# Delta-rule attention and feed-forward on one core: the first two chunks rebuilt

## The chip, the cores and the metric

The kernel runs on one core of a Trainium2 chip. The metric is the device time of one execution in microseconds; lower is better. The engines named below are TensorE (PE, with its weight loads as PEld), VectorE (DVE), ScalarE (ACT), GpSimd (POOL) and SyncE (SP). SP does no arithmetic here: it issues DMAs, in order, and a DMA that has to wait holds up those behind it. ACT and POOL issue some DMAs as well.

## What is computed

Two blocks follow each other. The first is a delta rule: for each of 4 batches and 8 heads a 48 x 48 state is carried over 768 tokens. The second is a feed-forward network on the 3072 tokens with all heads side by side (384 columns).

```python
k_n = k / (np.linalg.norm(k, axis=-1, keepdims=True) + 1e-06)
for t in range(S):
    y[:, :, t] = np.einsum('bhd,bhde->bhe', q[:, :, t], state)
    v_old = np.einsum('bhde,bhd->bhe', state, kt)
    state = state + bt[:, :, :, None] * np.einsum('bhd,bhe->bhde', kt, vt - v_old)
...
h = x @ w_in                                # 384 -> 2048
g = h * (1.0 / (1.0 + np.exp(-1.702 * h)))
return (g @ w_out).astype(np.float32)       # 2048 -> 384
```

The inputs q, k, v and beta are float32. The two weight matrices are float64 in DRAM, and the kernel turns them into float32 itself.

## The kernel before

**Tiling.** The 768 tokens are cut into 6 chunks of 128. A *unit* is one chunk of one batch with its 8 heads; there are 24, and unit n is chunk n // 4 of batch n % 4. Two neighbouring units (n even and n + 1) are a *pair*: they share one xT tile of 256 tokens, on which the feed-forward works.

**A unit's work.** `normalize` divides k by its norm (in the loop: squares, the power and the product on POOL, the rest on DVE). `prepare` transposes k on PE (psT, copied to kT), forms the products of all keys with all keys (psG, copied to G) and sends all of G, 512 KB, to DRAM (Nd). From there SP reads back the 32 x 32 blocks of the diagonal (NT), so that each (batch, head, block) lies on a lane of its own. `invert` turns these blocks into the inverses of unit lower triangular matrices by substitution on DVE: a multiplication with beta, 15 steps of a product and a reduction, then two groups of four larger products and reductions. The result goes to DRAM and back once more (Yd, XB). Chunk 0 is inverted for four units at once (128 lanes), the later ones a pair at a time (64 lanes). `scores` transposes q (psT, QS), multiplies it and the state with the keys (psQ), subtracts the state's part from V and masks the scores M on POOL.

**The chain.** The 128 tokens of a unit are four blocks of 32. `together` does one hop: `solve` multiplies the inverse of a block with V (psU, copied by ACT to US), and `below` subtracts a solved block from the blocks under it (psR, subtracted from V on DVE by `rest`). A hop handles a solve of one unit and a below of another, so two or three units are under way at once. `queries`, `outputs` and `state` make the output (psY) and the new state (ST). ACT copies the output to xT and `last`, and six SP DMAs move `last` into xT.

**Feed-forward.** `hidden` is x @ w_in with the activation (ph, gT), 16 pieces of three products a pair; `written` is g @ w_out (po, o, and a DMA to the output), 8 pieces of two products a unit. Both are generators; finished pairs are put into `queue`, and pieces are drawn from it between the steps of the attention. A piece has a cost of 1.3, and the share of a unit is 15.6 to 20.8.

**Weights.** The two words of a double are fetched into w_out's own space (or a spare tile) and made into a float by DVE and ACT (`from_double`), in parts of 512 columns for w_in and 384 for w_out. In the first units POOL issues most of these loads, as places become free.

**Order.** For units -1 to 5 `slot` runs six groups of steps (for units 2 to 5 with a scheduler's freedom on DVE, ACT and PE); from unit 6 on `woven` runs with the program's order held. `warm` issues products of a constant, whose results are not used. The names that the later text uses stand in these lines:

```python
for n in range(-1, len(units) + 1):
    in_order[0], now[0] = n < HB or n >= W, n
    step = slot if n < W else woven
    step(n, 15.6 if n <= B else 18.8 if n <= B + HB else 20.8)
run(take(1e9))
```

Of the kernel before, what the change touches and what calls it, by code (L numbers as in the profile page):

```python
# [18 lines left out]
def kernel(  # L19
# [33 lines left out]
    GR = 6  # L53
    NTH = HB * C
    FQ = 4
    GB = 4

    W0, W1, WB = 3, 1, (1, 3, 5, 7, 8)
    NA = W0

    NW, NA0, NY, NB0 = 80, 3, 48, 6
    XR = DP - D
    W = 6
    NS = C * C + C
    assert S % C == 0 and H == 8 and D <= DP and DM == H * D == KC * 128
    assert B == 4 and B * H * NB == 128 and FC == 4 * FQ
# [40 lines left out]
    in_order, now = [False], [0]  # L107

    class Engine:
# [5 lines left out]
        def __getattr__(self, name):  # L115
            op = getattr(self.engine, name)
            return pinned(op) if in_order[0] else op

    vec, act, pe = Engine(nc.vector), Engine(nc.scalar), Engine(nc.tensor)

    for i in range(B):
        nc.vector.memset(KN[i][:, :, D:DP], 0.0)
        load(i, ((KN, k),))

    bI = cpool.tile([128, NC, BS], F32, name="bI")
    betas = beta.rearrange("b h (c k j) -> (b h) c k j", k=NB, j=BS)
    for blk in range(NB):
        nc.scalar.dma_start(out=bI[blk::NB], in_=betas[:, :, blk, :])


    ident = cpool.tile([128, 128], F32, name="ident")
    make_identity(nc, ident)
    half = cpool.tile([128, H], F32, name="half")
    nc.gpsimd.memset(half, 0.5)

    nc.gpsimd.memset(YB, 0.0)
    nc.gpsimd.affine_select(
        out=YB, in_=YB, compare_op=ALU.not_equal, fill=1.0, base=0,
        pattern=[[1, BS], [-1, BS]], channel_multiplier=0,
    )  # L140


# [5 lines left out]
    def warm(n, after=None):  # L148

        ps = ps_moe.tile([128, 256], F32, tag="moe", name="ps_warm")  # L150
        if after is not None:
            after(ps[:, 0:1], 0.0)
        for _ in range(n):
            pe.matmul(ps, lhsT=ones[:, 0:128], rhs=ones, start=True, stop=True)  # L154

    warm(NW)
    table = cpool.tile([128, 1], F32, name="table")
    nc.scalar.activation(table, ident[:, 0:1], ACT.Copy)

    w_in = cpool.tile([128, KC, DFF], F32, name="w_in")  # L160
# [3 lines left out]
    nc.gpsimd.memset(low, -896.0 * (1 << 23))  # L164

    def from_double(dst, raw, n, alone):

        lo, hi = raw[:, :, 0], raw[:, :, 1]
        ts, stt = vec.tensor_scalar, vec.scalar_tensor_tensor
        if alone:
            ts, stt = pinned(ts), pinned(stt)
        AND, OR = ALU.bitwise_and, ALU.bitwise_or
        E1 = 1 << 20
        p = dst.bitcast(I32)  # L180

        ts(p, hi, 0x7FF * E1, None, op0=AND)
        if alone:
            ts(p, p, -896.0 * E1, 0.0, op0=ALU.add, op1=ALU.max)
            ts(p, p, 255.0 * E1, 8.0, op0=ALU.min, op1=ALU.mult)
        else:
            act.activation(p, p, ACT.Relu, scale=8.0, bias=low)
        yield
        t = wk.tile([128, n], I32, tag="P", name="tmp")
        f = t.bitcast(F32)  # L190
        ts(t, hi, E1 - 1, E1, op0=AND, op1=OR)
        stt(out=f, in0=lo.bitcast(U32), scalar=2.0**-32, in1=t, op0=ALU.mult, op1=ALU.add)
        stt(out=p, in0=hi, scalar=-(1 << 31), in1=p, op0=AND, op1=OR)
        stt(out=dst, in0=f, scalar=2.0**-20, in1=dst, op0=ALU.mult, op1=ALU.mult)
        yield

    N_IN = 512
    parts_in = KC * DFF // N_IN
    n_parts = parts_in + FC

    x_rows = [
        (ct * DP + o, (ct * NP + i) * D, m, step)
        for ct in range(2)
        for o, i, m, step in ((0, 0, D, D), (D, KC, XR, XR))
    ]

    stages, taken, made, begun = {}, {}, [], {}  # L210

    def stage(part):

        if part < parts_in:
            at = part % (2 * KC) * 2 * N_IN
            return at, at + 2 * N_IN
        f = part - parts_in
        if f >= FC - 2:
            return None
        depth = 2 if f < 2 or f >= 8 else 4  # L220
        if f >= 12:
            depth = 1
        at = FC * DM // (2 if f < 2 else 1) - (f % depth + 1) * 2 * DM
        return at, at + 2 * DM

    def together_with(part):

        return list(range(part, part + (KC if part < 3 * KC else 1)))

    def free(part):  # L230
        places = [s for p in together_with(part) if (s := stage(p)) is not None]
        return all(s[1] <= a or b <= s[0] for s in places for a, b in taken.values())

    def fetch(part, dma):

        if part < parts_in:
            j, f0 = part % KC, part // KC * N_IN
            parts = together_with(part)
            shape, src = (len(parts), N_IN), moe_w_in[:, f0 : f0 + N_IN]
            dst = w_in[:, j : j + len(parts), f0 : f0 + N_IN]  # L240
        else:
            parts = [part]
            shape, src = (1, DM), moe_w_out
            dst = target(part)
        if src.dtype != F32:
            if (s := stage(part)) is None:
                raw = wk.tile([128, *shape, 2], I32, tag="xT", name="raw", bufs=3)
            else:
                words = slice(s[0], stage(parts[-1])[1])
                raw = w_out.rearrange("p f d -> p (f d)")[:, words].bitcast(I32)  # L250
                raw = raw.rearrange("p (j n o) -> p j n o", j=shape[0], o=2)
            for i, p in enumerate(parts):
                stages[p] = raw[:, i]
                if s is not None:
                    taken[p] = stage(p)
            dst = raw.bitcast(src.dtype).rearrange("p j n o -> p j (n o)")
        if part < parts_in:
            for i in range(len(parts)):
                for p, r, m, step in x_rows:
                    dma(out=dst[p : p + m, i], in_=src[r + (j + i) * step : r + (j + i) * step + m])  # L260
        else:
            r = (part - parts_in) * 128
            dma(out=dst if src.dtype == F32 else dst[:, 0], in_=src[r : r + 128, :])
        return parts

    def target(part):
        if part < parts_in:
            j, f0 = part % KC, part // KC * N_IN
            return w_in[:, j, f0 : f0 + N_IN]
        return w_out[:, part - parts_in, :]  # L270

    def begin(part):

        if part not in begun:
            if part >= parts_in:
                a, b = (part - parts_in) * DM, (part - parts_in + 1) * DM
                if any(taken[p][0] < b and a < taken[p][1] for p in stages if p in taken):
                    return
            dst = target(part)
            begun[part] = from_double(dst, stages[part], dst.shape[-1], part < NA)  # L280
            next(begun[part])

    def convert(part):
        if part in stages:
            begin(part)
            if staged:
                begin(min(staged))
            stages.pop(part)
            next(begun.pop(part))

            made.append(part)
            while made and (len(made) > 1 or part < NA or part >= n_parts - 8):
                taken.pop(made.pop(0), None)

# [20 lines left out]
    def normalize_first(b0, nb=HB):  # L315

        tt, ts = pinned(vec.tensor_tensor), pinned(vec.tensor_scalar)
        red, recip = pinned(vec.tensor_reduce), pinned(vec.reciprocal)
        stt = pinned(vec.scalar_tensor_tensor)
        mult, add = ALU.mult, ALU.add  # L320
        z = wk.tile([128, 4, nb, H], F32, tag="ksq", name="z", bufs=1)
        x, y, t, s = (z[:, i] for i in range(4))
        for b in range(nb):
            K = KN[(b0 + b) % len(KN)][:, :, 0:D]
            sq = wk.tile([128, H, D], F32, tag="G", name="sq", bufs=6)
            tt(sq, K, K, op=mult)
            red(s[:, b], sq, axis=AX.X, op=add)
# [8 lines left out]
        recip(s, s)  # L336
        for b in range(nb):
            K = KN[(b0 + b) % len(KN)][:, :, 0:D]
            tt(K, K, s[:, b].broadcast_to([128, H, D]), op=mult)

    def transposed(src, dst, early=False):

        pool_, tag = (ps_seq, "seq") if early else (ps_big, "big")
        psT = pool_.tile([128, NP, 128], F32, tag=tag, name="psT")
# [5 lines left out]
    def prepare(n):  # L350

        c, b = units[n]
        kn = KN[n % len(KN)]
        kT = wk.tile([128, NP, 128], F32, tag="kT", name="kT", bufs=6)
        transposed(kn, kT, c == 0)
        yield 0.6
        G = wk.tile([128, H, 128], F32, tag="G", name="G", bufs=6)
        pool_, tag = (ps_moe, "moe") if c == 0 and b % 2 else (ps_big, "big")
# [10 lines left out]
        else:  # L369
            vec.tensor_copy(G[:, 1::2], ps[1])  # L370

        Nd = dram.tile([H * NS], F32, tag="Nd", name="Nd", bufs=4)
# [16 lines left out]
    def invert(c, b0=0, nb=B):  # L389
# [6 lines left out]
        if c == 0:  # L396
            tt, red = pinned(tt), pinned(red)
# [535 lines left out]
```

## Time and profile before

| what | value |
|---|---|
| median of 3 runs | 825.57 us (823.43 to 826.2) |
| the profiled execution | 821.86 us |
| its span, first to last instruction | 819.8 us |
| mean granted TensorE clock | 0.952 |
| DMA | 55.96 MB in 147698 packets |
| xT DMAs of unit 0 / of unit 1 issued on SP from | 94.09 us / 118.27 us |
| dummy products on PE (`ps_warm`) | 152 + 108 |
| po, 128 x 384 | 704 + 64 records, two for each product |

How to read it: the busy share of an engine is a mean over the whole span, and stages with different limits are mixed in it. A matmul's record has its latency in it, so the price of one is better taken from a long row of them. An idle engine costs nothing unless others wait for it. The line number of a group is often that of a helper (L105 holds the program's order), so groups are told apart by their tiles.

### The profile page before, as it was taken

To read this page: it belongs to the slowest core of one execution; us is meant where nothing else is said; L and a number is where in the kernel's file an instruction comes from. 1 tells how busy PE (TensorE), PEld (TensorE's weight loads), DVE (VectorE), ACT (ScalarE), POOL (GpSimd) and SP (SyncE) were. 2 spreads that over 40 slices of the span, in tenths; PEclk is the share of its full clock that TensorE was granted. 3 is DMA by queue.
4 is the path that set the end of the run, shared out by engine and by line. 5 is a ranking of instruction groups with operands and counts; after the bars stand their busy time and mean duration, and the time that the engine had idled before them with its cause. 6 is when DMAs were issued, how large, how long until landed. Compare 5 with 4: busy or idle time off the path is not lost.

```text
span 819.8 us, 18780 instructions
## 1 busy us (share of the span) xinstructions
PE 768.8 (94%) x8100; PEld 577.4 (70%) x8100; DVE 483.0 (59%) x1037; ACT 230.7 (28%) x499; POOL 131.7 (16%) x138
## 2 busy tenths in 40 slices
PE   8429799889799999999999999999999999999998
PEld 7327688557676876867867867867768768677684
DVE  7797989787965675666667667666656730100000
ACT  2212543242232332322422322322322223212120
POOL 2013120322021222122123122212201000000000
PEclk9659889978979999999999999999999999999999
DMA  7986732721315123214204213213222020000000
GB/s 146 199 183 122 201 87 82 178 68 48 68 30 125 34 49 96 60 23 100 62 21 102 53 32 90 54 43 80 53 59 45 12 51 1 11 16 1 24 1 19
DMA packets 147698, 55.96 MB, mean 68 GB/s; under 512 B 114720, under 2 KB 143616, under 8 KB 147616
## 3 DMA queue, kind: packets, MB, share of 16 engines
q1 hardware_dynamic: 139872, 41.96, 24.0%
q0 software_dynamic: 2752, 10.62, 4.7%
q10 hardware_dynamic: 4992, 2.20, 1.0%
q8 instruction: 63, 1.03, 0.6%
q14 instruction: 19, 0.16, 0.1%
HBM read 33.13 MB, written 20.45 MB: 65 GB/s over the span
## 4 chain that ended last, share of the span: by engine, by line
PE 79%; DVE 6%; issue 6%; DMA 4%; SPq 2%; POOL 1%; ACT 1%; DVEq 0%; POOLq 0%; ACTq 0%
PE po L105 28%; PE ph L105 25%; PE psY L105 5%; PE psU L105 4%; PE psQ L105 3%; PE ps_warm L154 3%; PE ph L633 2%; PE psG L105 2%; PE psR L105 2%; DMA w_out<-in_moe_w_out_dram 2%; PE psT L105 1%; SPq L105 1%; DMA w_out<-in_moe_w_in_dram 1%; DVE tmp L105 1%; PE psG L362 1%
## 5 line engine op out<-in xcount | busy, mean ns | idle before, releaser
L105 PE MATMUL po<-w_out,gT 128*128 128x384 f32 x704 | 239.3, 490 | 0.0
L105 PE MATMUL ph<-xT,w_in 128*128 128x256 f32 x966 | 222.0, 384 | 0.3
L105 PEld LDWEIGHTS ph<-xT,w_in 128*128 128x128 f32 x966 | 180.3, 191 | 30.9 <-issue 2.3
L105 PEld LDWEIGHTS po<-w_out,gT 128*128 128x128 f32 x704 | 130.1, 190 | 82.6 <-issue 1.9
L105 DVE TENSOR_TENSOR V<-V,psR 64x384 f32<-64x384 f32 (+1 forms) x80 | 44.4, 556 | 194.8 <-PE psR L105 194.0
L105 DVE TENSOR_TENSOR P<-NT,YB 64x18 f32<-64x18 f32 (+25 forms) x171 | 82.3, 481 | 4.5
L105 ACT ACTIVATE gT<-ph 128x512 f32<-128x512 f32 x81 | 48.2, 595 | 115.9 <-PE ph L105 115.8
L105 DVE TENSOR_REDUCE YB<-P 64x6 f32<-64x18 f32 (+25 forms) x171 | 72.7, 425 | 5.5
L105 ACT COPY US<-psU 32x384 f32<-32x384 f32 x80 | 37.6, 470 | 131.9 <-PE psR L105 118.4
L528 POOL TENSOR_SCALAR_AFFINE_SELECT M<-M 128x1024 f32<-128x1024 f32 x24 | 29.8, 1240 | 226.6 <-DVE M L105 159.8
L105 PEld LDWEIGHTS psU<-V,XB 32*32 32x32 f32 x1280 | 45.9, 105 | 27.9 <-issue 20.5
L105 PE MATMUL psU<-V,XB 32*32 32x48 f32 x1280 | 54.3, 203 | 2.1 <-DVE V L105 2.1
L105 PE MATMUL psR<-US,G 32*32 32x48 f32 x1920 | 52.8, 203 | 0.0
L633 PE MATMUL ph<-xT,w_in 128*128 128x128 f32 (+1 forms) x282 | 47.0, 321 | 1.6 <-DMA xT<-last 1.6
L105 PEld LDWEIGHTS psR<-US,G 32*32 32x32 f32 x1920 | 44.6, 105 | 0.5 <-issue 0.5
L633 PEld LDWEIGHTS ph<-xT,w_in 128*128 128x128 f32 x282 | 40.3, 198 | 5.7 <-issue 2.4
L154 PE MATMUL ps_warm<-ident 128*128 128x256 bf16 x152 | 22.8, 318 | 16.7 <-DVE ps_warm L105 14.4
L90 POOL DMA_DIRECT2D KN<-in_k_dram x14 | 13.4, 955 | 153.1 <-PE psY L105 102.0
L308 POOL TENSOR_TENSOR rn<-ssq,half 128x8 f32<-128x8 f32 x17 | 36.9, 2169 | 2.9 <-DVE ssq L306 2.9
L105 ACT COPY o<-po 128x384 f32<-128x384 f32 x22 | 10.5, 479 | 77.7 <-PE po L105 55.8
L154 PEld LDWEIGHTS <-ident 128*128 128x128 bf16 x152 | 17.1, 114 | 21.0 <-issue 14.6
L105 DVE TENSOR_TENSOR P<-NT 64x256 f32<-64x256 f32 (+7 forms) x36 | 30.3, 841 | 0.3
(144 smaller groups left out, 871.0 us busy)
## 6 DMA issues: line engine op xcount, KB each, us to landing
Nd<-G SPq DMA_DIRECT2D x20, 512.0 KB, 3.5
w_out<-in_moe_w_out_dram POOLq DMA_DIRECT2D x14, 384.0 KB, 3.7
QP<-in_q_dram SPq DMA_DIRECT2D x24, 192.0 KB, 3.9
V<-in_v_dram SPq DMA_DIRECT2D x24, 192.0 KB, 3.0
out_dram<-o SPq DMA_DIRECT2D x24, 192.0 KB, 1.9
w_out<-in_moe_w_in_dram SPq DMA_DIRECT2D x18, 192.0 KB, 5.2
NT<-Nd SPq DMA_DIRECT2D x24, 128.0 KB, 2.6
Yd<-YS SPq DMA_DIRECT2D x24, 128.0 KB, 2.5
```

The lines of the kernel that those rows point to most:

```text
L90: dma(out=dst[n % len(dst)][:, :, 0:D], in_=src[b, :, c * C : (c + 1) * C, :].rearrange("h p d -> p h d"),)
L105: return lambda *a, **kw: tc.keep_in_program_order(op(*a, **kw))
L154: pe.matmul(ps, lhsT=ones[:, 0:128], rhs=ones, start=True, stop=True)
L308: nc.gpsimd.tensor_tensor(rn, ssq, half, op=ALU.pow)
L362: pe.matmul(ps[h % 2][:, h // 2], lhsT=kT[r, h // 2, :], rhs=kT[r, h // 2, :], start=True, stop=True,)
L528: nc.gpsimd.affine_select(out=self.M, in_=self.M, compare_op=ALU.is_gt, fill=0.0, base=0, pattern=[[0, H], [1, 128]], channel_multiplier=-1,)
L633: pe.matmul(ph[:, u], lhsT=w_in[:, j, f * 128 : (f + 1) * 128], rhs=xT[:, j, t], start=(j == 0), stop=(j == KC - 1),)
```

## The change

The steps up to unit 8 are written out by hand, and the program's order is held for them on PE, DVE, ACT, POOL and SP. From unit 7 on `woven` runs as before. In detail:

- The keys of all four units of chunk 0 are normalized in one go. Their squares are made by ACT.
- For chunk 0 only the diagonal blocks of the key products are formed first (psD, 32 x 32, in `diagonal`) and sent through DRAM, a quarter of the bytes; G is formed afterwards and stays on the chip.
- Chunk 1 is inverted for its four units at once, on 128 lanes, as chunk 0 is.
- Units 0 and 1, then 2 and 3, 4 and 5, 6 and 7 run as pairs of chains (`hops`): eight hops, in which one unit's solve stands beside the other's below. Between the hops stand pieces of feed-forward (`feed`) and of conversion (`fill`).
- The conversion works on pieces of 768 columns (256 of w_in for all three parts, or two parts of w_out), then of 384. Loads are issued by SP (in part by POOL for the first two quarters of w_in) when a named piece is done.
- x @ w_in of units 0 to 3 comes first; g @ w_out begins when all weights are converted.
- `spend` keeps no debt while the queue of feed-forward is empty. ACT makes the copies for which it shared the work with DVE.
- gT has eight buffers where it had four; spare ones hold some of the tiles of the first units.

```diff
+    def diagonal(b, D_):
+        kT = kTs[b]
+        ps = [ps_seq.tile([128, NP, BS], F32, tag="seq", name="psD") for _ in range(2)]
+        for h in range(H):
+            r = slice(h % 2 * 64, h % 2 * 64 + D)
+            for blk in range(NB):
+                u = slice(blk * BS, (blk + 1) * BS)
+                pe.matmul(
+                    ps[h % 2][u, h // 2, :], lhsT=kT[r, h // 2, u], rhs=kT[r, h // 2, u],
+                    start=True, stop=True,
+                )
+        for e in range(2):
+            act.activation(D_[:, e::2, :], ps[e], ACT.Copy)
...
+    fetches = {
+        ("in", 1): lambda: fetch_in(2),
+        ("in", 3): lambda: fetch_in(3),
+        ("in", 5): lambda: (fetch_out(0), fetch_out(1)),
+        ("in", 7): lambda: (fetch_out(2), fetch_out(3), fetch_out(4), fetch_out(5)),
+        ("out", 3): lambda: (fetch_out(6), fetch_out(7), fetch_out(9), fetch_out(12)),
+        ("out", 5): lambda: fetch_out(8),
+        ("out", 7): lambda: (fetch_out(10), fetch_out(11), fetch_out(13)),
+        ("out", 9): lambda: fetch_out(14),
+        ("out", 12): lambda: fetch_out(15),
+    }
...
     def spend(cost):
-        debt[0] += cost
+        debt[0] = debt[0] + cost if queue else 0.0
...
+    for b in range(B):
+        sync(
+            out=NT[b * NB * H : (b + 1) * NB * H].rearrange("d i k -> d (i k)"),
+            in_=Nds[b].rearrange("(d r) -> d r", r=BS * BS),
+        )
...
+    fill(8)
+    for b in range(B):
+        gram(b)
+        warm(NA)
+    pair = [new_step(n) for n in range(B)]
+    inverting = invert(0)
...
+    run(inverting)
+    fill(5)
+    def hops(a, b):
+        yield [(a, 0)], []
+        for blk in range(NB - 1):
+            yield [(b, blk)], [(a, blk)]
+            yield [(a, blk + 1)], [(b, blk)]
+        yield [(b, NB - 1)], []
...
+    path = hops(*pair[:2])
+    for i in range(2 * NB):
+        together(*next(path))
+        fill(1)
+    for s in pair[:2]:
+        put_out(s)
+        fill(2)
...
+    ffn.append(hidden(xTs[0], gTs[0], slice(0, NTH), 1.3))
+    path = hops(*pair[2:])
+    for i in range(2 * NB):
+        together(*next(path))
+        feed()
+        fill(2)
+    for s in pair[2:]:
+        put_out(s)
+        feed()
+        fill(2)
...
+    for n in range(B, 2 * B):
+        for _ in keys(n):
+            feed()
+            fill(3)
+    requests(3)
+    while len(ffn) > 2:
+        feed()
+        fill(3)
+    run(converting)
+    inverting = invert(1)
+    pair = [new_step(n) for n in (B, B + 1)]
+    for i in range(20):
+        ahead_of(inverting, 1 + i % 4 // 3)
+        feed()
...
+    run(inverting)
+    for n in (8, 9):
+        for _ in keys(n):
+            feed(1 if n == 8 else 0)
...
+    chain(*pair, lambda i: feed())
+    enqueue(2)
...
+    def more(i):
+        ahead_of(inverting, 1)
+        feed(2)
+    chain(*pair, more)
+    enqueue(3)
...
+    queue.extend(ffn)
+    for n in range(7, len(units) + 1):
+        woven(n, 20.8)
     run(take(1e9))
```

## The prediction

> **What bounds the kernel now.** I read the page's busy times and slices first, then a table of stages, then the chain of waits, and the order of instructions of both programs last.
>
> ```profile
> span 819.8 us, 18780 instructions
> PE 768.8 (94%) x8100; PEld 577.4 (70%) x8100; DVE 483.0 (59%) x1037; ACT 230.7 (28%) x499; POOL 131.7 (16%) x138
> PE   8429799889799999999999999999999999999998
> DVE  7797989787965675666667667666656730100000
> PEclk9659889978979999999999999999999999999999
> ```
>
> TensorE is full from about 230 us on. Before that VectorE is the fuller engine and TensorE is partly kept warm by dummy products. The table by stage (columns: PE, PEld, DVE, ACT, POOL busy, clock, DMA share, GB/s):
>
> ```profile
> 0.00:67.00 67.00, 38.04 (x295) 30.74 (x296) 56.93 (x138) 15.67 (x32) 12.70 (x31) 0.72 0.96 177
> 67.00:112.00 45.00, 39.03 (x679) 32.84 (x677) 36.93 (x83) 21.70 (x43) 11.30 (x17) 0.89 0.63 154
> 112.00:176.00 64.00, 57.00 (x690) 42.18 (x689) 57.00 (x123) 22.83 (x54) 13.93 (x18) 0.97 0.40 101
> 176.00:230.00 54.00, 48.57 (x456) 36.98 (x457) 43.41 (x100) 15.93 (x33) 6.52 (x6) 0.82 0.28 63
> 289.00:347.00 58.00, 57.89 (x655) 43.44 (x654) 35.96 (x77) 17.11 (x39) 11.41 (x10) 1.00 0.26 62
> ```
>
> In the last row two units take 58 us and VectorE has 36 us of work in them (40 in the 59 us before). That number decides below. The chain of waits fixes the rest of the run, and the price of feed-forward work:
>
> ```profile
> 398.55 2.07 PE psY L105 x48
> ...
> 775.08 20.72 PE ph L105 x96
> 795.80 20.66 PE po L105 x64
> ```
>
> 398.55 is unit 10's output; 421.25 us follow, all TensorE-bound. 20.72/96 and 20.66/64 make a piece of feed-forward work (three products of ph, or two of po) 1.29 us, and a pair's feed-forward 41.4 us. The start, from the timeline, SP's queue and the DMA table:
>
> ```profile
> 31.00 1.22 DVE L105 TENSOR_TENSOR NT<-NT,bI 128x1024 f32<-128x1024 f32 x1 [3.11 <-DMA NT<-Nd]
> 57.97 7.58 PE L154 MATMUL ps_warm<-ident 128*128 128x256 bf16 x48 [14.36 <-DVE ps_warm L105]
> 67.44 0.86 PE L105 MATMUL psU<-V,XB 32*32 32x48 f32 x16
> 69.65 0.88 PE L105 MATMUL psR<-US,G 32*32 32x48 f32 x48
> 70.58 1.14 DVE L105 TENSOR_TENSOR V<-V,psR 32x384 f32<-32x384 f32 x2 [0.57 <-PE psR L105]
> 39.34 16.68 SPq L105 DMA_DIRECT2D w_out<-in_moe_w_in_dram  x24
> 118.27 4.59 SPq L617 DMA_DIRECT2D xT<-last  x6
> Nd<-G SPq DMA_DIRECT2D x20, 512.0 KB, 3.5
> NT<-Nd SPq DMA_DIRECT2D x24, 128.0 KB, 2.6
> xT<-last SPq DMA_DIRECT2D x66, 16.0 KB, 1.8
> ```
>
> The reader is to see: the inversion runs from 31.0 to 57.9; the first solve comes at 67.4; an SP issue costs 0.7 to 0.8 us.
>
> [...] clock digits 6 and 5 in slices 2 and 3, where TensorE waits. [...] Here 16 KB lands in 1.8 us, 128 KB in 2.6. [...] Here 48 psR records over three column groups take 0.88 us, as 16 psU records of one tile do (0.86). I use it for psD, which no row shows.
>
> **The change part by part**, on the clock of the profiled run.
>
> *1. To the first solve.* One normalization of four units instead of two of two: K tiles land about 1.4 us apart (TensorTensor at 4.14 waits, the next at 5.55), so the last at some 8.3 (estimate); squares on ACT, reduces 0.55, thirteen small operations at 0.21, a reciprocal, four multiplications at 0.52: about 15.0. TensorE leaves its 80 warm products at 13.9 as before. Per unit psT 0.45 and psD: 64 records over four column groups, 1.0 us at psR's rate, 3.2 us if serial as psU is; I take 1.0. The last block copy ends at 20.8 (before: last G 23.2). Nd is a quarter of the size; I take 2.5 us, and 2.6 for NT: the inversion starts at 26.0 (31.0 before). Same 25.5 us on 128 lanes, so 51.5. YS, Yd, XB (1.2+2.5+2.7) lie inside the 51 warm products that follow (8.0 us): first solve at 60, before 67.4. Gain 7.5; with serial psD -1.
>
> *2. Units 0 and 1.* A hop is 0.8 us of TensorE, then 0.12+1.1 (two V subtractions) or 0.12+0.55, and 0.25 to restart. Eight hops: 1.6+2x2.3+4x1.73+1.6 = 15, to 75. One conversion operation of 768 columns (0.69x1.5 = 1.03, estimate) fits beside each hop. Outputs end at 77.7.
> *The wait it adds:* the last conversion of hop 8 frees quarter 3's place, and its 12 loads stand ahead of the six xT copies on SP (12x0.69 = 8.3). So xT is issued at 83.3, not 77.5, and the first ph is complete 6.9 us later (118.27 to 125.18 before): 90.3. Behind that ph TensorE holds units 2 and 3. Stall 11.
>
> *3. Units 2 and 3 with feed-forward.* Per hop VectorE has subtractions plus two conversions, 2.2 to 3.1 us; TensorE 0.8+1.29. VectorE is later: 17 us, plus two outputs and feeds 5: 112.
>
> *4. Conversion and keys of units 4 to 7.* Left on VectorE: one 768 operation, a piece of 3.7, two of 4.1, eight 384 pieces at 2.25, four normalizations at 1.0: 35 us. The loads of w_out are 384 KB each (3.7 us to landing), fetched when a piece is done, on one SP queue with four Nd and NT that each hold it 3.5 us. I follow them: waits at the fourth pair (about 4), at f=8 (3), at 10, and at 15, together 9. End 156. TensorE's 35 us of ph and psG hide here. The keys of unit 7 end 4 us later; Nd 3.7, NT 2.6: inversion of all four at 166.
>
> *5. The second inversion:* 26.6, V subtractions 2.2, YS 1.2: 196. 52 po (33.6 us) and 7 us of scores hide beside it. But TensorE's order has psG of unit 9 ahead of the solve; its keys go reduce, pow (2.17), reciprocal, multiply, for 8 and then 9, psT, kT, psG: 10.5 us. XB needs 4.7. So 206.5; behind that psG stand the whole chain of units 4 and 5 and its outputs. ACT is held too: its copy of YB for the inversion (about 13 us in) stands ahead of unit 1's o copy and the QS copies, but the two po banks carry TensorE over it.
>
> *6. Units 4 and 5:* 8 hops with 1.29 each, 16.6; outputs to 226.6; feed-forward is used up, so xT (6.9) is waited for in full: 233.8. *Units 6 and 7:* scores and pieces 7.2, chain 16x1.29+8x0.8 = 27.1, outputs: 272.
>
> *7. Feed-forward of pairs 2 and 3.* TensorE-bound: 54 po, 48 ph, 5 psT, 3 psG, 2 psQ, 3 hops = 34.9+20.7+2.3+3.3+2.8+2.4 = 66.4, to 339.
>
> *8. The queue is dry.* In the new TensorE order no ph or po stands between there and unit 9's output: 2 2/3 units of attention alone (20 us of TensorE). VectorE's own work bounds them: 11 us for the rest of unit 8's turn, then 20 and 18 (36 to 40 a pair in the table), and about 3 of waits; then xT 5: 52, so 392 (339.4+52.5). If only the chain counted it would be 34; with halved clock 60.
>
> *9.* To unit 10's output, 33 ph, two hops, psT, psY: 17.5, and 3 for the clock after the pauses: 412. Feed-forward done there: 225 ph and 128 po; before 171 wide and 96 half-wide ph (219 wide) and 128 po. So the rest is 421.25 less 2.6 = 418.7. Sum: 412.4+418.7 = 831.1 against 819.8, so 11.3 slower. No step after unit 10 changes.
>
> Unpriced edits cost nothing: fewer warm products, memsets on POOL and betas on SP lie under the first loads; POOL's half of the w_in loads is 12 issues of 0.56 at a time when POOL waits.
>
> The profiled run took 821.86, 2.06 outside the span; the median shown, 825.57, is 3.7 above it. The difference is added to the median: 836.9, forecast 837.
>
> **Rivals.**
> *A, SP's queue is not waited for* (faster). Steps 2 and 4 charge SP 6+9 us, and step 6 about 2 more for issues. If DMAs are issued as fast as elsewhere (xT 0.58 median) and w_out lands ahead of use, 17 us go: 820. For it: 3.7 us of landing is short against 2.3 to 4 us per piece, with four fetched ahead. Against: 24 loads took 16.68 us on this queue. It decides once over 11 of the 17 are absent.
> *B, the clock is lost.* 164 warm products instead of 260, and pauses of over 4 us at 78, 156, 200, 227 and in the dry stretch. If the clock halves for the 13 us that follow three of them with TensorE full, and through two chains (16 hops at +0.6), 3x6+9 = 27 come on top, less the 3 counted: 861. For it: digits 7, 8 and 7 between 164 and 246 us before. Against: VectorE is the later engine in most of these places.
> *C, the account does not run dry* and feed-forward fills step 8: 837-30 = 807. The order printed for the new TensorE program speaks against it; under 3 in 100.
>
> **How the numbers follow.** Forecast 0.50 (its own range 828 to 847), A 0.25, B 0.22, C 0.03. A measurement tells about 0.3%, 2.5 us. A lies at 820 with part of it around 825: faster 0.22, same 0.08; slower 0.70. The range takes A's upper part and B's lower: 817 to 860.
>
> **What would show it.** Right: NT at 26, first psU at 60, first ph near 90, second NT at 166, a gap without ph and po of some 52 us near 340, unit 10's psY near 412. Each step's own time tests it. Wrong: a dry stretch under 41 us, or the second chain starting before 195: then it is faster.

## The result

The changed kernel takes 859.69 us (median of four runs, 855.94 to 865.49), the kernel before 825.34 beside it: a ratio of 1.043, 95% interval 1.036 to 1.049. That is 34 us slower where 11 were forecast: the direction is the forecast one, 859.69 lies inside the range by 0.3 us, and the size is three times what the sum gave. A few executions of a kernel are over 1.5% slower than its fastest, at a lower clock (in run 10 841.34 us at a mean of 0.929, the fastest 819.0 at 0.956); the ratios leave these out, and below only two executions each of the last two versions in run 10 are known to be such. The profiled execution took 858.35 us (before: 821.86). From its page, with the slices of 21.4 us:

```profile
span 856.5 us, 18794 instructions
PE 782.2 (91%) x8164; PEld 584.3 (68%) x8164; DVE 451.7 (53%) x905; ACT 237.5 (28%) x511; POOL 119.5 (14%) x121
PE   7777788996979999955899999999999999999998
DVE  4695777584124445688666766666666651100000
PEclk9566998999699999955899999999999999999999
```

TensorE was full from 230 us on before. Now it has two more holes: the digits 6, 9 and 7 between 193 and 257 us, and 5, 5 and 8 between 364 and 428 us. In both the clock digits fall too. VectorE has 31 us less work in all, and is nearly idle in the first hole (digits 1 and 2 from 214 to 257 us). The table by stage, with one stretch of the kernel before as its last line (PE, PEld, DVE, ACT, POOL busy, clock, DMA share, GB/s):

```profile
200.00:218.00 18.00, 10.46 (x53) 6.64 (x51) 1.98 (x7) 3.17 (x6) 4.92 (x4) 0.79 0.48 106
218.00:250.00 32.00, 27.26 (x454) 18.09 (x452) 6.58 (x13) 7.68 (x19) 0.00 (x0) 0.82 0.17 40
293.00:361.00 68.00, 67.01 (x384) 47.40 (x382) 40.70 (x80) 17.20 (x37) 17.09 (x13) 1.00 0.32 71
361.00:419.00 58.00, 36.55 (x679) 31.03 (x679) 46.08 (x93) 15.40 (x35) 12.37 (x11) 0.59 0.25 58
361.00:419.00 58.00, 57.89 (x656) 43.49 (x655) 36.34 (x78) 16.49 (x37) 12.51 (x10) 1.00 0.26 62
```

Where the lead went can be read from the busy time of ph and po alone, summed over such tables (some of it at the halved clock). Until 250 us the changed kernel has done 100.5 us of feed-forward and the kernel before 88.5; until 361 us it is 187.5 against 171.0. From 361 to 419 it does 0.2 us and the kernel before 43.6, and at 437 it is 25.5 us behind (202.7 against 228.2). From unit 10's psY on, both programs need nearly the same time (419.1 us, and 421.25 before). So the change does fetch feed-forward early, and then has none left where VectorE holds the attention.

### The profile page after: what moved, and what is told of

Its sections match the earlier page's. It is cut to its first block, busy times and chain, and to the rows that moved or that the text cites. A ratio compares the mean times of both kernels' runs of the same rounds, so it can differ in the third digit from the quotient of the medians.

```text
span 856.5 us, 18794 instructions
## 1 busy us (share of the span) xinstructions
PE 782.2 (91%) x8164; PEld 584.3 (68%) x8164; DVE 451.7 (53%) x905; ACT 237.5 (28%) x511; POOL 119.5 (14%) x121
## 3 DMA queue, kind: packets, MB, share of 16 engines
q1 hardware_dynamic: 146192, 49.47, 25.9%
## 4 chain that ended last, share of the span: by engine, by line
PE 73%; DVE 4%; DMA 2%; ACT 2%; POOL 1%; issue 1%; SPq 0%; POOLq 0%; ACTq 0%; DVEq 0%
PE po L102 29%; PE ph L102 24%; PE psY L102 5%; PE psU L102 5%; PE psQ L102 3%; PE psG L102 3%; PE psT L102 2%; PE psR L102 2%; DVE P L102 1%; DMA Nd<-G 1%; DVE YB L102 1%; DMA NT<-Nd 1%; POOL rn L102 1%; DVE NT L102 1%; ACT QS L102 0%
## 5 line engine op out<-in xcount | busy, mean ns | idle before, releaser
L102 PE MATMUL ph<-xT,w_in 128*128 128x256 f32 x1152 | 269.4, 389 | 9.2 <-DMA xT<-last 8.9
L102 PE MATMUL po<-w_out,gT 128*128 128x384 f32 x768 | 265.5, 496 | 0.0
L102 PEld LDWEIGHTS psU<-V,XB 32*32 32x32 f32 x1536 | 68.1, 114 | 46.5 <-issue 27.7
L102 DVE TENSOR_TENSOR P<-NT,YB 64x8 f32<-64x8 f32 (+31 forms) x190 | 89.7, 472 | 5.7 <-DVE YB L102 0.3
L102 PE MATMUL psU<-V,XB 32*32 32x48 f32 x1536 | 80.3, 215 | 12.3 <-DVE P L102 6.3
L102 DVE TENSOR_REDUCE YB<-P 64x4 f32<-64x8 f32 (+31 forms) x190 | 81.0, 426 | 6.5
L102 PE MATMUL psQ<-QS,kT 48*128 48x176 f32 (+1 forms) x384 | 39.7, 354 | 4.1 <-ACT QS L102 4.0
L102 PE MATMUL psG<-kT 48*128 48x128 f32 x384 | 35.3, 336 | 4.7 <-ACT kT L102 4.5
L102 PEld LDWEIGHTS psQ<-QS,kT 48*128 48x128 f32 x384 | 33.0, 218 | 9.3 <-ACT QS L102 7.8
L102 PEld LDWEIGHTS psG<-kT 48*128 48x128 f32 x384 | 30.0, 235 | 10.7 <-ACT kT L102 6.4
```

Source lines behind the costliest of these rows:

```text
L102: return lambda *a, **kw: tc.keep_in_program_order(op(*a, **kw))
```

## The forecast's steps beside the trace

All in us on the clock of the profiled run; the last column is what each step added to the error.

| step | mark | forecast | trace | added |
|---|---|---|---|---|
| 1 | first operation of the inversion | 26.0 | 30.59 | +4.6 |
| 1 | first solve | 60 | 66.25 | +1.7 |
| 2 | first ph complete | 90.3 | 94.2 | -2.4 |
| 3, 4 | units 2, 3 out; second inversion starts | 112; 166 | 115.9; 169.9 | 0.0 |
| 5 | YS of the second inversion done | 196 | 200.2 | +0.3 |
| 5 | chain of units 4 and 5 starts | 206.5 | 218.0 | +7.3 |
| 6 | first ph behind that chain complete | 233.8 | 250.0 | +4.7 |
| 6 | unit 7's outputs | 272 | 292.6 | +4.4 |
| 7 | feed-forward of pairs 2 and 3 used up | 339 | 361.2 | +1.6 |
| 8 | ph again | 391.9 | 419.4 | +5.3 |
| 9 | psY of unit 10 | 412.4 | 437.35 | -2.6 |
| 9 | from there to the end | 418.7 | 419.1 | +0.4 |

The keys of units 8 and 9, step by step in the timeline (VectorE, ScalarE, GpSimd and TensorE together):

```profile
208.78 1.09 ACT L102 ACTIVATE G<-psG 128x512 f32<-128x512 f32 x2 [2.66 <-PE psG L102]
209.75 0.52 ACT L102 ACTIVATE ksq<-KN 128x384 f32<-128x384 f32 x1
210.30 0.55 DVE L102 TENSOR_REDUCE ssq<-ksq 128x8 f32<-128x384 f32 x1 [7.40 <-ACT ksq L102]
213.31 0.83 POOL L102 TENSOR_TENSOR KN<-KN,rn 128x384 f32<-128x384 f32 x1 [0.68 <-DVE rn L102]
214.19 1.12 PE L102 MATMUL psT<-ident,KN 128*128 128x128 f32 x4 [3.96 <-POOL KN L102]
```

The square of unit 9 (ksq) needs only its loaded keys, but it stands on ScalarE behind the copies of kT and G for unit 8. VectorE waits 7.4 us for it, and the first solve of units 4 and 5 stands behind unit 9's psG.

## Experiments

Theory when they were chosen: the loss has three parts, the empty account from 361 to 419 us, the serial keys and the chain without feed-forward from 200 to 250, and the start. Rivals: the halved clock sets these stretches; or TensorE's work is only shifted, so nothing comes back. Each edit is against the changed kernel. The runs were made in four groups, with the kernel before beside each (medians 823.15 to 824.39 us), and the changed kernel only once, ahead of them; through the ratios to the kernel before, the gains below come out up to 2.3 us smaller. The times of runs 1, 4 and 5 overlap those of the changed kernel (855.94 to 865.49), so what these three show is read from stretches of their profiles, one profile each.

**1. Spread what is left over units 7 to 10**

```diff
-        woven(n, 20.8)
+        woven(n, 7.2 if n < 11 else 20.8)
```

> Only the shares change: units 7 to 10 are given 7.2 of feed-forward each instead of 20.8, so that the 22 pieces left at that point last until unit 10. Theory (the dry stretch is VectorE's work, and TensorE work laid under it is free): the stretch from unit 7 to unit 10 shrinks by most of 22 x 1.29 = 28 us, unit 10's psY comes at about 413 instead of 437 and the time is 836 (830 to 841). Rival (the attention chain itself, slowed by the halved clock, sets 20 us a unit, and a piece lengthens it by its own time): psY stays at 432 to 438, time 854 to 860.

Measured 854.71 us (852.81 to 856.31), psY of unit 10 at 435.3: 5 us of the 28. The theory fell in this form; the numbers are those of its rival.

**2. The same, with one piece a hop in units 6 and 7**

```diff
-        feed(2)
+        feed()
...
-        woven(n, 20.8)
+        woven(n, 9.75 if n < 11 else 20.8)
```

> As the run with new shares, and one piece instead of two in each hop of units 6 and 7; the 8 pieces saved there go to units 7 to 10 as well (share 9.75). Theory: a hop of units 6 and 7 falls from 3.6 us to about 2.5, 8 us less there, and the 8 pieces hide under VectorE later: 828 (822 to 834). Rival (they only move the load): no better than the run with new shares alone.

Measured 840.88 us (839.89 to 842.01): 19 us, of which 8.5 lie between psY of units 4 and 7 (43.4 us for 51.9), as expected; the whole misses the range that was expected (822 to 834). From psY of unit 7 to that of unit 10 there are eight pieces more than in run 1, in less time (133.7 us for 141.8). The stretches of both that lie alike, run 1 first:

```profile
335.00:385.00 50.00, 39.55 (x462) 26.94 (x466) 41.37 (x92) 11.87 (x25) 11.24 (x8) 0.76 0.23 54
```

```profile
330.00:371.00 41.00, 36.79 (x473) 27.52 (x477) 37.24 (x79) 12.86 (x27) 10.35 (x8) 0.96 0.27 61
```

VectorE is busy for 0.83 of run 1's stretch and 0.91 of run 2's; TensorE has about as much busy time in both, but in run 1 at a mean clock of 0.76. I read it so: thinly spread pieces left pauses (TensorE is idle for 10.5 of the 50 us in run 1 and 4.2 of the 41 in run 2), the clock was lower beside them, and the pieces then took longer in front of the next hop (at half clock a piece takes 2.9 us for 1.6 in the chain of units 4 and 5). That reading rests on one profile of each, and that the pauses are what lowered the clock is not shown. In run 2 TensorE is busy 123 of the 134 us from 285 to 419, so units 7 to 10 can take little more.

**3. Dummy products in the dry stretch** (the call stands at four places of a step; one is shown)

```diff
+    def keep(n):
+        if n in (9, 10):
+            warm(16)
...
+        keep(n)
         spend(share / 6)
```

> Sixteen dummy products (1.8 us at full clock) at four places of the steps of units 9 and 10, in TensorE's pauses, nothing else changed: the clock should stay up in the dry stretch. Theory (VectorE's own work bounds the stretch): 2 to 5 us less, 855 to 858. Rival (the halved clock bounds it): the stretch falls from 58 to below 49 us, 850 or less.

Measured 859.59 us (856.53 to 862.73). The same stretch in the table:

```profile
361.00:418.00 57.00, 45.76 (x805) 36.94 (x806) 47.41 (x93) 15.39 (x35) 13.34 (x11) 0.82 0.25 60
```

The clock goes from 0.59 to 0.82, and without ph and po it still lasts 57.3 us (58.2). Without the edit VectorE is busy in 46 of the 58 us and waits in the rest, so a higher clock could take some 12 us off at most; about 1 came off. The test isn't quite clean, since the dummy products take TensorE 20.2 us themselves: VectorE's waits for psY and psG fall from 6.9 to 3.1 us, but those for psR rise from 2.6 to 5.6. What is shown is that VectorE's own work sets most of the stretch; a few us of the clock may be hidden behind the dummy products. Beside run 1: the low clock (0.59) cost little here, about 1 us, where TensorE had nothing else to do, and seems to cost where pieces are there (0.76 in run 1's stretch).

**4. The keys of units 8 and 9 beside the hops of units 4 and 5**

```diff
-    for n in (8, 9):
-        for _ in keys(n):
-            feed(1 if n == 8 else 0)
...
-    chain(*pair, lambda i: feed())
+    first, second = keys(8), keys(9)
+    order = ((first,), (first,), (first, second), (second,), (first, second), (first,), (second,), (second,))
+
+    def beside_keys(i):
+        for k in order[i]:
+            next(k)
+        feed()
+
+    feed(3)
+    chain(*pair, beside_keys)
```

> The keys of units 8 and 9 are prepared beside the hops of units 4 and 5 instead of ahead of them; everything else as in the changed kernel. Theory (the serial key steps at 200 to 218 are a stall on the path): the chain of units 4 and 5 starts at about 205 instead of 218, the hops keep feed-forward beside them, and the time falls by 10 to 14 us to 846 to 850. Rival (the stall is only moved: feed-forward saved there runs dry in the later stretch just as long): 857 to 860.

Measured 855.94 us (851.27 to 858.42). From the start of YS to the first solve it is 6.5 us for 19.0 before the edit: the stall is gone. But the chain now carries psT and psG of both units and eight pieces for six (psY of unit 4 comes 25.9 us after the solve, for 20.6), and the later dry stretch is as long as it was (57.2). By the medians about 4 of 12.5 us are kept, between what the theory and the rival said.

**5. The keys of both units step by step together, in their old place**

```diff
-    for n in (8, 9):
-        for _ in keys(n):
-            feed(1 if n == 8 else 0)
+    for _ in zip(keys(8), keys(9)):
+        feed()
```

> The changed kernel with one edit: the keys of units 8 and 9 are prepared step by step together instead of one after the other, in the same place, so that on ScalarE the square for unit 9 no longer stands behind the copies of kT and G for unit 8. Theory (the 17.8 us that the keys take are two serial passes, of which 7.4 us is VectorE's wait for that square): the chain of units 4 and 5 starts 6 us earlier against the end of the second inversion, 853 to 855. Rival (GpSimd's pow and multiply, each some 2 us and one after the other, hold the keys anyway): 1 us or less gained, 858 to 860.

Measured 855.41 us (852.28 to 861.4). From the start of YS to the first solve 16.0 us for 19.0. VectorE's wait for the square is gone:

```profile
202.38 0.55 DVE L102 TENSOR_REDUCE ssq<-ksq 128x8 f32<-128x384 f32 x1 [0.59 <-ACT ksq L102]
206.02 1.12 PE L102 MATMUL psT<-ident,KN 128*128 128x128 f32 x4 [3.44 <-POOL KN L102]
213.05 0.49 PE L102 MATMUL psG<-kT 48*128 48x128 f32 x2 [0.68 <-ACT G L102]
```

7.4 us less of waiting gave 3 on the path: GpSimd's steps (3.44) and unit 9's psG, which now waits for the G copies of unit 8, come next. Both accounts of the 17.8 us were partly right. In this profile the chain behind it also ran at full clock. It has the same work in the changed kernel (the first line) and here, from the first solve to psY of unit 4:

```profile
218.00:238.60 20.60, 19.91 (x350) 12.61 (x348) 4.44 (x8) 4.85 (x10) 0.00 (x0) 0.77 0.17 44
216.10:232.20 16.10, 15.41 (x345) 9.96 (x344) 4.44 (x8) 3.76 (x8) 0.00 (x0) 1.00 0.27 67
```

Runs 1, 2 and 3 have the changed kernel's program up to there: 18.1 us at a mean clock of 0.88 to 0.89. So TensorE bounds this chain, and the clock sets its time.

**6. The start: w_in's first quarter loaded later**

```diff
-    fetch_in(0, other_queue)
     for i in range(B):
         pool.memset(QP[i][:, :, D:DP], 0.0)
...
+    fetch_in(0, other_queue)
     fetch_in(1, other_queue)
...
-    fill(8)
...
     run(inverting)
-    fill(5)
+    fill(13)
```

> The loads of the first quarter of w_in are issued behind those of q and v instead of at the very start, and its eight conversion operations come after the inversion. Theory (TensorE's pauses of 3.03 and 1.86 us inside the groups psT and psD, ended by nothing but issue, come from the weight loads that fill the DMA engines at that moment): the pauses go, the last copy of a diagonal block is at 20 instead of 24.4, and the inversion starts at 26 instead of 30.6; the eight operations then cost 7 us before the first solve, so 858 to 864. Rival (the dense run of small products outruns TensorE's own instruction supply): both pauses stay at 3 and 2 us, inversion at 30 to 31, 864 to 870.

Measured 858.47 us (857.94 to 861.0). TensorE's timeline of the changed kernel and of this one:

```profile
19.82 0.59 PE L102 MATMUL psT<-ident,KN 128*128 128x128 f32 x2 [3.03 <-issue]
20.34 1.63 PE L102 MATMUL psD<-kT 48*32 48x32 f32 x126
23.82 0.26 PE L102 MATMUL psD<-kT 48*32 48x32 f32 x2 [1.86 <-issue]
```

```profile
17.92 0.38 PE L102 MATMUL psT<-ident,KN 128*128 128x128 f32 x2 [1.69 <-issue]
21.66 0.26 PE L102 MATMUL psD<-kT 48*32 48x32 f32 x2 [1.80 <-issue]
```

The first pause is 1.3 us shorter here, the second about the same, and both stay at the same instruction. The length of the first says nothing of the loads, though: in the eleven profiles whose program is the same up to there (the changed kernel's and those of all other runs but run 7) it is anything from 0 to 4.4 us, and the second 1.3 to 2.1. What lies outside these profiles is when the inversion starts, 28.54 us for 30.6 to 31.9. The conversions that were moved behind it take the gain back (psY of unit 0 at 82.2, for 81.5).

**7. psG between the groups psD**

```diff
         Nds.append(Nd)
+        gram(b)
...
-    for b in range(B):
-        gram(b)
-        warm(NA)
+    warm(NA)
```

> The score products psG of units 0 to 3 are moved between the groups psD, which dilutes the run of 256 small products without changing their number. Theory (TensorE takes the small products faster than they are brought to it): the two pauses of 3.0 and 1.9 us fall below 1 us in sum. Rival (a pause belongs to a place in the program or to the loads that are under way): they stay 1.7 us or more each. The total is not what this run is for; within 5 us of 859.

One run, 866.58 us; the inversion starts at 34.08 us, since psG now stands ahead of it. One pause is left:

```profile
20.33 0.29 PE L102 MATMUL psD<-kT 48*32 48x32 f32 x13 [2.98 <-issue]
```

It comes after 223 records of TensorE's products counted from the start of the program, where the changed kernel's first comes after 222; the second is gone. Neither account holds alone. In the changed kernel the two pauses are 2 + 126 = 128 records apart, 256 instructions with their weight loads. The page lists a DMA queue of its own for instructions:

```profile
q8 instruction: 64, 1.05, 0.5%
q14 instruction: 18, 0.15, 0.1%
```

The first is 64 packets of 16 KB. Together the two queues moved 1.20 MB, and the page counts 18794 instructions: by estimate from these figures about 64 bytes for an instruction in the mean, and some 256 to a packet of 16 KB, as many as lie between the two pauses. Such packets begin at 17.20 and 21.48 us in the changed kernel, 15.06 and 19.04 in run 6, and 17.87 in this run. In these and in the ten other profiles every one of these pauses, long or short, ends 2.2 to 2.9 us after one begins; other packets pass without a pause (24.96 in the changed kernel and 21.44 here, where TensorE has larger products). My guess is that TensorE ran out of instructions at the seam of two packets, because 128 records of psD take only 1.6 us. Neither whose instructions a packet holds nor where in the program it ends is shown, so this is a reading of times that fit; no run took the seam away.

**8. Dummy products at units 0 to 3**

```diff
         together(*next(path))
+        warm(4)
         fill(1)
...
         together(*next(path))
+        if i == 0:
+            warm(22)
         feed()
```

> Dummy products only: 4 beside each hop of units 0 and 1, 22 behind the first hop of units 2 and 3, where TensorE waits for xT; nothing else changed. Theory (the clock that the pauses cost is on the path here, since hops and first pieces run at half rate between 67 and 110 us): hops of units 0 and 1 fall from 1.9 to 1.5 us, the first pieces run at full rate, 5 to 9 us less, 851 to 855. Rival (VectorE's conversion bounds both stages, as it bounds the dry stretch): 858 to 861.

Measured 861.38 us (860.08 to 862.58): no gain, as the rival said. But at units 0 and 1 the run is no test of the theory, because the clock hardly rose there. From the first solve to psY, the changed kernel first:

```profile
66.25:81.50 15.25, 10.07 (x321) 8.82 (x320) 10.34 (x15) 5.06 (x9) 0.00 (x0) 0.64 0.47 98
66.54:84.50 17.96, 16.14 (x353) 11.68 (x352) 10.88 (x15) 5.53 (x10) 0.00 (x0) 0.68 0.50 106
```

The dummy products stand between the hops themselves, 18.0 us for 15.3. In the changed kernel the products of five of the eight hops run at half clock (it is at half from 70.6 to 84.3; 1.5 us for 0.9), and VectorE waits 0.6 to 0.9 us for psR in three of these. By estimate (5 x 0.6) up to 3 us lie there, which no run got back. At units 2 and 3 the changed kernel's profile had full clock already, so there was nothing to gain. Run 1's, with the same program up to there, did not (from the first complete ph to psY of unit 2, the changed kernel first):

```profile
94.30:111.40 17.10, 16.47 (x346) 12.66 (x346) 15.50 (x21) 8.60 (x13) 0.00 (x0) 0.99 0.35 74
94.40:116.70 22.30, 22.30 (x349) 16.92 (x348) 16.08 (x22) 9.05 (x14) 0.00 (x0) 0.70 0.27 57
```

At 0.70 TensorE is busy throughout, and the stage is 5 us longer. So here the clock is on the path, and it differs between executions of the same steps.

**9. Level account and keys together, some pieces kept**

Runs 2 and 4, and

```diff
         ahead_of(inverting, 1 + i % 4 // 3)
-        feed()
+        feed(i % 4 < 3)
...
     chain(*pair, beside_keys)
+    feed(4)
     enqueue(2)
```

> The level account (one piece a hop in units 6 and 7, share 9.75 in units 7 to 10), the keys of units 8 and 9 beside the hops of units 4 and 5, and five pieces of the second inversion kept for the pauses before the chain of units 4 and 5 and before their xT. Theory: 19 from the level account and 4 to 12 from the keys and the kept pieces add up: 828 (824 to 836). Rival (what is moved out of one stage is missing in the next, the same TensorE work is only shifted): 838 to 842, as with the level account alone.

Measured 825.75 us (17 runs, 822.3 to 832.88), ratio to the kernel before 1.004 (1.002 to 1.007). That is 34 us below the changed kernel and 11 more than runs 2 and 4 gave singly (19 and 4): the second inversion, with five pieces fewer beside it, takes 26.5 us for 29.1, and the kept pieces fill the wait for xT, which was 11.1 us without ph or po. How much of the 11 is theirs was not separated. The table:

```profile
200.00:212.00 12.00, 5.69 (x87) 3.50 (x85) 1.38 (x2) 0.89 (x2) 0.00 (x0) 0.72 0.46 89
212.00:234.00 22.00, 22.00 (x376) 14.66 (x376) 6.66 (x15) 8.46 (x18) 4.93 (x4) 1.00 0.24 66
234.00:272.00 38.00, 38.00 (x550) 29.33 (x541) 19.03 (x49) 13.27 (x33) 3.00 (x3) 1.00 0.31 49
358.00:380.00 22.00, 19.98 (x358) 13.69 (x346) 20.28 (x37) 6.68 (x16) 6.03 (x5) 1.00 0.27 67
```

TensorE is full from 212 to 272 us, and only 200 to 212, the wait for XB, stays half empty.

**10. Three further sizes**

Run 9 with dummy products as in run 8 and the loads of v and q for units 4 to 6 moved behind the keys of units 4 to 7:

> The run before with the dummy products of the clock run, and with the loads of v and q for units 4 to 6 put behind the keys of units 4 to 7 on SP's queue. Theory: 5 to 9 from the clock and 3 from w_out landing sooner on top: 817 (812 to 824), below both kernels. Rival (VectorE bounds these stages): within 3 us of the run before.

Measured 827.48 us (821.89 to 833.35): the rival.

Run 9 with seven pieces ahead of the chain of units 4 and 5, one piece in every second hop, and thinner keys of units 10 and 11:

```diff
-        feed()
+        feed(i % 2)
...
-    feed(3)
+    feed(7)
...
-            feed(2)
+            feed()
...
-        woven(n, 9.75 if n < 11 else 20.8)
+        woven(n, 13 if n < 11 else 20.8)
```

> The level account and the keys beside the hops (the run at 825.75), with three sizes changed: seven pieces instead of three ahead of the chain of units 4 and 5, where TensorE still waited 6.7 us for XB, and one piece only in every second hop of that chain; one piece instead of two at each of the ten steps of the keys of units 10 and 11, with the share of units 7 to 10 at 13 instead of 9.75. Theory (what is left are pauses of 6.7 us at 200 and about 8 us between 300 and 358, both filled by work taken from stages where TensorE is full): 816 (812 to 820), faster than before. Rival (the stages are TensorE-bound in sum, and a piece moved only moves): 823 to 828.

Measured 828.05 us (median of all 22 runs, 824.21 to 836.85). psY of unit 6 comes at 263.4 (268.7 in run 9), and it is all given back, as the rival said: with one piece a step TensorE waits for the keys of units 10 and 11,

```profile
277.86 0.66 PE L102 MATMUL psT<-ident,KN 128*128 128x128 f32 x4 [3.37 <-POOL KN L102]
...
289.21 0.81 PE L102 MATMUL psT<-ident,KN 128*128 128x128 f32 x4 [2.95 <-POOL KN L102]
```

and units 7 to 10 take 141.6 us for 133.8 from psY of unit 7 to that of unit 10.

The same without the last two hunks:

> The level account with the keys beside the hops (825.75), and only the change ahead of the chain of units 4 and 5: seven pieces instead of three there, one piece in every second hop; the keys of units 10 and 11 keep two pieces a step and the share stays 9.75. Theory (the pause of 6.7 us before XB is filled with work that a hop then need not carry): unit 6's psY at 263 as in the finer version instead of 269, and with the keys of units 10 and 11 undisturbed 820 to 822, some 3 us below the kernel before. Rival (the gain is given back in units 7 to 10): 825 to 828.

Measured 822.75 us (median of all 22 runs) against 824.39 for the kernel before: a ratio of 0.998 (0.996 to 1.000). It lies between the two expectations, is the fastest version tried, 37 us below the changed kernel, and can't be told from the kernel before. Its one profile is of the longest of the 22 executions (841.34 us), so where unit 6's psY comes in the others isn't known.

## Why the forecast came out as it did

*Right:* what the change turns on. There is a stretch without feed-forward before unit 10, VectorE's own work sets most of its length (run 3), the rest after unit 10 is 419.1 us (418.7), and stage 4 and the second inversion took what steps 4 and 5 said within 0.3 us. Stage 4 agrees in its sum only: VectorE waited 4.6 us for w_out instead of 9, and 4.3 us for squares, powers and psY, which the sum left out.

*Wrong in size.* The steps that failed are terms of the sum: the keys in step 5, the hops at full clock in step 6, the addition in step 8, and the start:

- Step 5, "10.5" for the keys of units 8 and 9: 17.8 us from YS to the first solve of units 4 and 5, +7.3. I let unit 9's steps follow unit 8's product at once, and counted psT, kT and psG only once. ScalarE's order sets unit 9's square behind unit 8's copies of kT and G. Taking that order away gave 3 us on the path in run 5's profile; that the rest is two passes through GpSimd and ScalarE is read from the timeline, not shown by a run.
- Step 6, "16.6" for the hops of units 4 and 5: 20.6, +4 of the +4.7. The clock was at half from 214.0 to 227.6, after TensorE had waited 3.96 us up to 214.2; a psU with psR then takes 1.49 us instead of 0.87 and a piece 2.9 instead of 1.6. VectorE has only the subtractions beside it, so this is on the path, and at full clock the chain takes 16.1 us (run 5), as forecast. Rival B had this term. At units 0 and 1 the 15 us were met (15.3) by luck: the four hops put at 1.73 us took 2.2 each, and the two put at 2.3 took 1.5 and 2.2.
- Step 6, units 6 and 7, +4.4: 16 pieces and 8 hops took 28.8 us to psY for 27.1, and the rest is spread over scores and outputs.
- Step 8: the terms written there (11, 20, 18, 3 and 5) add up to 57, not to the 52 that was carried on. The slip is nearly all of the +5.3. That 57 would have been close to the 58.2 us measured is in part luck: VectorE's work is 46.1 for the 49 put, and the waits are 12 for "about 3" and the 5 for xT. (Step 7 has a slip the other way: 272 and 66.4 make 338.4, not 339.4.)
- Step 1, +6.3: 4.9 us of pauses inside psT and psD, which no part of the sum had; psD itself, the unknown there, took 0.76 us for the 1.0 I chose. The rest is the inversion, 27.5 us for 25.5.
- Step 2's wait was forecast for the wrong reason: the 12 loads took SP 5.4 us for 8.3, its queue was clear at 86.5, and xT was itself ready only at 87, because the outputs took 4.2 us for 2.7.

The sum of the errors is 25 us, and 23 us on the medians. The time lies at rival B's 861, but not for B's reasons. B charged 18 of its 27 us to three pauses and put 13 us at half clock in full work behind each, which was my estimate; where feed-forward begins again, at 91 and at 247, the clock is at half only from 91.1 to 94.5 and from 248.1 to 251.5, and at 419 it is full. The other 9 us, in two chains, came in part: 4 at units 4 and 5, and by estimate up to 3 at units 0 and 1, which the luck there hides. Rival A had a point in stage 4 (4.6 us of waits for 9) and at xT, but the time went there all the same. C didn't happen.

*Why slower at all* is answered by run 9: the same rebuilt chunks, with the account spent otherwise and the keys beside the hops, take 825.75 us. The time was lost to where the pieces were spent, and to what stood in front of the second chain, not to the diagonal blocks or the conversion. That the rebuilt start gives no gain even then (0.4% slower) is measured; which of its parts takes back the lead of 12 us at 250 was not separated.

## What to carry to other kernels

When work that fills TensorE is brought forward, draw up where it is spent, stage by stage, against the busy time of the engine that bounds each stage: what is spent where TensorE is full anyway is missing where another engine is late. Keep a few pieces for each known wait (here XB and xT), and don't expect a thin spread to be as good as a dense one: in run 1's thin stretch the mean clock was 0.76, in run 2's dense one 0.96 (one profile each). Don't judge a clock experiment before the trace shows that the clock rose (in run 8, at units 0 and 1, it went from 0.64 to 0.68 only). Price a preparation of two units by walking each engine's order across both, not by one unit's chain.

## What was not expected of the hardware

- TensorE paused with no wait shown at two instructions 128 records apart, 0 to 4.4 us at the first and 1.3 to 2.1 at the second in eleven profiles, in a run of 256 small records that takes 64 of them in 0.76 us. However long the pause, it ended 2.2 to 2.9 us after a 16 KB instruction packet began. The hops of the chains, 64 records in 0.87 us, show such pauses more rarely: one of 1.6 us in run 8 and one of 1.8 in run 7.
- The clock stayed at half for 27.3 us (364.1 to 391.4) with TensorE busy in 18.4 of them, and an edit that raised the clock of the stretch from 0.59 to 0.82 left its time within 1 us (57.3 for 58.2).
- psY of unit 2 comes anywhere from 111 to 118 us in the profiles of kernels that are the same up to there. In the early ones the first hops behind the wait for xT run at full clock, in the late ones at half (17.1 and 22.3 us in the two shown in run 8).
